# Splitting the even rows of a sequence DFT by s mod 4, and running the DFT sums on zeroed or seeded PSUM banks

## The chip, the cores and the metric

One core of a Trainium2 chip (trn2). The metric is the device time of the core in microseconds, median of several executions. "Step n" below is the n-th of the kernel's 376 equal work steps, counted from 0; it begins with the first TensorE record `H<-Rr,Wc` of that step in the trace. In the profile PE is TensorE and PEld its weight loads, DVE is VectorE, ACT ScalarE, POOL GpSimd, and SPq the queue in which SyncE issues DMAs; `H<-Rr,Wc` means that tile `H` is written from `Rr` and `Wc`. PSUM is the memory that matmuls add into; a bank is one tile of 512 columns of it.

## The reference, cut to what matters

```python
def _attn_ref(x):                      # x: (8, 3008, 256)
    X = np.fft.fft(x, axis=1)          # the s-DFT: over 3008 rows
    X = np.fft.fft(X, axis=2)          # over 256 channels
    return X.real.astype(np.float32)

def _moe_ref(x, w_in, w_out):          # (24064,256), (256,2048), (2048,256)
    h = x @ w_in
    g = h * np.cos(h)
    return (g @ w_out).astype(np.float32)
```

The output is `_moe_ref` of the reshaped `_attn_ref`. The channel DFT is folded into `w_in` at the start of the kernel. What is left per batch is a real and an imaginary DFT over the rows, for even and odd output indices: four "DFTs" (R even, I even, R odd, I odd), each from operands folded by the symmetries of the cosine and the sine.

## The kernel before: the parts that the change touches

Each of 376 steps has 11 fp32 matmuls of 256 columns on TensorE, at least five VectorE operations, seven ScalarE operations and four GpSimd sums (`sum_1` to `sum_4`, of which the third product on bank `pB` needs `sum_2`). In between lie, batch by batch, the loads of `x`, the folds on GpSimd, and the four DFTs, each in two halves (even and odd rows of the folded sequence).

```python
    def load_x(b):                       # [four tiles of 128 partitions x 6 rows]
        for j in (2, 1):                 # reversed row order: a gather by an index table
            c = 1 if j == 2 else 2 if b == NB - 1 else 0
            nc.gpsimd.indirect_dma_start(out=L[j], in_=xflat,
                in_offset=bass.IndirectOffsetOnAxis(ap=ix[:, c : c + 1], axis=0), ...)
        nc.sync.dma_start(out=L[0], in_=xrows(b, 0, 6, 128))
        nc.sync.dma_start(out=L[3], in_=xrows(b, HALF, 6, 128))
    # [...]
    def dft_mms(ps, ri, kodd, par, stat, width):
        n = NO if kodd else NE           # 376 or 377 outputs
        for t in range(3):
            m = 2 * t + par
            c = par * BW + t * NE
            mm(ps[:, 0:n], stat[:, m * width : m * width + 128],
               MC[ri, kodd][:, c : c + n], t == 0, t == 2)   # start flag, stop flag

    def set_rest(ps, n):                 # the zero matmul behind each half
        mm(ps[:, n:512], zero[:, 0:128], zero[:, 0 : 512 - n], False)
    # [...]
    class Dft:
        def copy(self):                  # ScalarE: odd half out of PSUM
            act(self.bs[0:M, 0:n], self.pb[0:M, 0:n])
        def plus(self):                  # VectorE: ring <- odd + even half
            vtt(self.ring[0:M, sl], self.bs[0:M, a:z], self.pa[0:M, a:z], ALU.add)
        def minus(self):                 # VectorE: reversed ring <- even - odd half
            ...
    # [...]
    def load_ext(j):                     # channel 128 of all rows, element by element
        copy(...)                        # 8 x 768 elements of 4 bytes, SyncE queue
        nc.sync.dma_start(out=xe_dr[j], in_=t[:, 0:768])
    def get_ext():                       # and back in runs of six
        for j in range(4):
            nc.sync.dma_start(out=xs[:, j], in_=xe_dr[j].rearrange("b (p m) -> p b m", m=6))
    # [...]
    def at_half(step, d, par, col):      # where a half stands in the schedule
        def run():
            d().ps = bank("H")
            d().mms(par, d().ps)
            set_rest(d().ps, d().n)
        at(t + 4.75, run)
        # odd: copy at t+T+1.46; even: plus, minus at t+T+1.01
```

The banks `H` are shared with the main steps, where ScalarE writes the channel-128 term into the bank and the matmuls add to it without a start flag. A DFT half starts with the start flag, and a zero matmul on the columns behind it follows. Without these zero matmuls the numbers come out wrong (before_no_zero below: relative error 0.24); the reading is that the start flag makes TensorE forget that those columns had been written.

## Time and profile before

| | before |
|---|---|
| time, median of the 3 runs | 2002.85 us (2000.21 to 2002.99) |
| profiled span | 1999.9 us, granted TensorE clock 0.997 |
| PE / DVE / ACT / POOL busy | 99 / 70 / 72 / 67% |
| step 0 begins / steps 28 to the end | 38.9 us / 1815.5 us |

From the page of before, part 1 (busy us, share of the span, instructions) and part 4 (the chain of waits that ended last, by engine):

```profile
PE 1975.4 (99%) x8842; PEld 1648.6 (82%) x8842; DVE 1406.9 (70%) x2278; ACT 1431.2 (72%) x2729; POOL 1336.8 (67%) x1842
...
PE 92%; DVE 2%; issue 2%; ACT 1%; POOL 1%; DMA 1%; DVEq 0%; POOLq 0%; SPq 0%; ACTq 0%
```

TensorE is the bound. Its busy time can't be added up, because the records of pipelined matmuls overlap; the starts can. The timeline of before around one DFT half, TensorE alone (start, length, engine, line, operation, tiles, shapes, count):

```profile
1008.08 0.59 PE L229 MATMUL pD<-G,w 128*128 128x256 f32 x2
1008.51 2.06 PE L229 MATMUL H<-MC,o 128*128 128x376 f32 x6
1010.51 0.23 PE L229 MATMUL H<-zero 1*128 1x136 bf16 x1
1010.66 1.13 PE L229 MATMUL H<-Rr,Wc 128*128 128x256 f32 x4
```

An fp32 matmul is two records. Two of 256 columns go from 1008.08 to 1008.51, 216 ns each; six of 376 columns and the wait for the zero matmul take 2.00 us. Read record by record, a DFT record takes 316 ns, but 409 where the zero matmul follows; the zero matmul 157; the first record behind it 320 instead of 216. That is 93 + 157 + 104 = 354 ns for one zero matmul of 136 columns: its own weight load and that of the fp32 matmul behind it are not hidden (in the trace they start within 4 ns of their matmuls, the other loads about one record earlier).

GpSimd behind a gather of before, timeline:

```profile
181.93 1.00 POOL L288 TENSOR_TENSOR o<-xl 128x381 f32<-128x381 f32 x1
183.20 0.96 POOL L142 DMA_INDIRECT xl<-in_x_dram,ix  x1 [0.27 <-DVE G L598]
184.18 3.03 POOL L238 TENSOR_TENSOR G<-G 128x256 f32<-128x256 f32 x4
```

A gather stands right behind the fold that frees its buffer and holds the four sums of the step back. TensorE's waits for GpSimd in before, from the list of waits (total us, times, longest):

```profile
PEld pB L229 <- POOL G L238: 13.3, 38, 1.0
...
PE pB L229 <- POOL G L238: 1.8, 6, 0.6
```

So there were small waits already.

### The profile page before, as it was taken

What the parts mean: (1) busy time and instruction counts of PE and PEld (TensorE: products, weight loads), DVE (VectorE), ACT (ScalarE), POOL (GpSimd) and SP (SyncE); (2) the same over time, 40 slices, a digit from 0 to 9 for tenths busy, and PEclk for the clock granted to TensorE, in tenths of its full rate; (3) what the DMA queues carried; (4) which work ended last, traced back from release to release, by engine and by line L of the source; (5) the groups of instructions that cost most, each with busy time, mean ns of one, the idle gap of its engine ahead of it and who ended that gap; (6) DMA issues with size and microseconds to landing.
All of it is one profiled execution on the core that took longest, in us unless ns stands there. A gap on an engine that the chain in (4) does not pass through costs nothing.

```text
span 1999.9 us, 27874 instructions
## 1 busy us (share of the span) xinstructions
PE 1975.4 (99%) x8842; PEld 1648.6 (82%) x8842; DVE 1406.9 (70%) x2278; ACT 1431.2 (72%) x2729; POOL 1336.8 (67%) x1842
## 2 busy tenths in 40 slices
PE   8999999999999999999999999999999999999997
PEld 4878888888888888888788888888888888888886
DVE  5776667766677666777677766777667766677776
ACT  2777667776677767777677766777667876677775
POOL 3777657776677756777567865778647776555654
PEclk9999999999999999999999999999999999999999
DMA  9712100211002110130101301013000100001101
GB/s 309 6 34 76 22 12 19 56 41 19 11 19 69 24 23 11 20 83 9 22 18 18 80 9 22 11 28 81 9 16 11 30 19 10 13 11 16 18 11 22
DMA packets 252139, 66.90 MB, mean 33 GB/s; under 512 B 242194, under 2 KB 245034, under 8 KB 251482
## 3 DMA queue, kind: packets, MB, share of 16 engines
q1 hardware_dynamic: 249578, 52.53, 14.4%
q0 software_dynamic: 2416, 12.61, 1.9%
q8 instruction: 70, 1.15, 0.2%
q14 instruction: 75, 0.61, 0.1%
HBM read 40.26 MB, written 24.80 MB: 33 GB/s over the span
## 4 chain that ended last, share of the span: by engine, by line
PE 92%; DVE 2%; issue 2%; ACT 1%; POOL 1%; DMA 1%; DVEq 0%; POOLq 0%; SPq 0%; ACTq 0%
PE H L229 38%; PE pB L229 16%; PE pC L229 16%; PE pD L229 15%; PE pA L229 8%; DVE G L598 1%; POOL G L238 1%; ACT G L241 1%; DVE G L235 0%; DMA wex<-wx 0%; DMA wx<-Ws 0%; ACT E L241 0%; DVE v L235 0%; DVE M L235 0%; POOL xl L142 0%
## 5 line engine op out<-in xcount | busy, mean ns | idle before, releaser
L238 POOL TENSOR_TENSOR G<-G 128x256 f32<-128x256 f32 x1504 | 1079.6, 728 | 619.1 <-DVE G L598 532.5
L598 DVE SCALAR_TENSOR_TENSOR G<-H,G 128x512 f32<-128x512 f32 x376 | 257.4, 685 | 309.1 <-ACT G L241 309.1
L235 DVE TENSOR_TENSOR G<-H,G 128x512 f32<-128x512 f32 x376 | 260.1, 692 | 222.8 <-ACT G L241 219.7
L241 ACT ACTIVATE E<-H 128x512 f32<-128x512 f32 x376 | 224.2, 596 | 261.1 <-PE H L229 257.9
L229 PE MATMUL H<-Rr,Wc 128*128 128x256 f32 x1504 | 393.1, 384 | 4.7 <-ACT H L241 4.6
L241 ACT ACTIVATE G<-H 128x512 int32<-128x512 f32 x376 | 224.5, 597 | 239.3 <-DVE G L235 236.1
L229 PE MATMUL H<-Ir,Ws 127*128 127x256 f32 x1504 | 388.6, 380 | 1.4 <-ACT E L241 1.4
L229 PE MATMUL pC<-G,WT 128*128 128x256 f32 x1504 | 387.0, 379 | 0.6 <-DVE u L235 0.4
L241 ACT ACTIVATE H<-Rb,wex 128x256 f32<-128x256 f32 x752 | 360.2, 479 | 25.8 <-DMA wex<-wx 6.5
L229 PEld LDWEIGHTS H<-Rr,Wc 128*128 128x128 f32 x1504 | 280.0, 190 | 49.7 <-ACT H L241 7.4
L229 PEld LDWEIGHTS H<-Ir,Ws 127*128 127x128 f32 x1504 | 283.0, 190 | 45.6 <-ACT E L241 7.1
L229 PEld LDWEIGHTS pC<-G,WT 128*128 128x128 f32 x1504 | 284.3, 189 | 42.8 <-PE H L229 2.5
L241 ACT ACTIVATE G<-G,halfpi 128x512 f32<-128x512 f32 x376 | 269.1, 716 | 0.3 <-DVE G L235 0.3
L235 DVE TENSOR_TENSOR G<-E,H 128x512 f32<-128x512 f32 x376 | 255.9, 681 | 3.4 <-issue 2.0
L235 DVE TENSOR_TENSOR M<-G,M 128x512 f32<-128x512 f32 x376 | 257.7, 685 | 0.0
L598 DVE SCALAR_TENSOR_TENSOR G<-G,M 128x512 f32<-128x512 f32 x376 | 254.5, 677 | 0.4 <-ACT M L241 0.3
L241 ACT ACTIVATE M<-M,halfpi 128x512 f32<-128x512 f32 x376 | 245.9, 654 | 0.3 <-DVE M L235 0.2
L229 PE MATMUL pB<-G,WT 128*128 128x256 f32 x752 | 227.5, 384 | 1.9 <-POOL G L238 1.8
L229 PE MATMUL pA<-G,w 128*128 128x256 f32 x752 | 223.7, 379 | 0.9 <-PE H L229 0.9
L241 ACT ACTIVATE M<-G 128x512 int32<-128x512 f32 x376 | 224.4, 597 | 0.0
L229 PE MATMUL pD<-G,WT 128*128 128x256 f32 x752 | 223.8, 379 | 0.0
L229 PE MATMUL pD<-G,w 128*128 128x256 f32 x752 | 223.7, 379 | 0.0
(111 smaller groups left out, 1762.2 us busy)
## 6 DMA issues: line engine op xcount, KB each, us to landing
out_dram<-ot SPq DMA_DIRECT2D x504, 32.0 KB
xl<-in_x_dram SPq DMA_DIRECT2D x16, 768.0 KB
MC<-dft_mats SPq DMA_DIRECT2D x4, 1131.0 KB
out_dram<-ot SPq DMA_DIRECT2D x256, 2.0 KB
Rb<-r SPq DMA_DIRECT2D x10, 376.0 KB
w<-in_moe_w_in_dram SPq DMA_DIRECT2D x4, 512.0 KB
w<-in_moe_w_out_dram SPq DMA_DIRECT2D x1, 2048.0 KB
out_dram<-ot SPq DMA_DIRECT2D x64, 28.0 KB
```

What stands on the lines that cost most here:

```text
L229: nc.tensor.matmul(out_, lhsT=lhsT, rhs=rhs, start=start, stop=stop, skip_group_check=True)
L235: pin(nc.vector.tensor_tensor(out=o, in0=a, in1=b, op=op))
L238: pin(nc.gpsimd.tensor_tensor(out=o, in0=a, in1=b, op=op))
L241: pin(nc.scalar.activation(out=o, in_=i, func=func, **kw))
L598: nc.vector.scalar_tensor_tensor(out=o, in0=h, scalar=TWO_PI, in1=c, op0=ALU.mult, op1=ALU.mult)
```

## The change

Intent: (1) the even half of each DFT is split once more, by s mod 4, so that 189 outputs are computed for each of two blocks and the rest come by adding and subtracting: 4 matmuls of 189 columns in place of 3 of 377. (2) No start flag on `H` banks: the even half runs on a bank that VectorE zeroed, the odd half on a bank that ScalarE seeded with the unfolded even half, so the sum comes out of PSUM directly, and the zero matmuls go. (3) For that the rows lie differently on the partitions: runs of four rows, and runs of two, so each load becomes two or three.

```diff
+def _row_of(m):
+    p = np.arange(128)
+    return 4 * p + m if m < 4 else 512 + 4 * (p % 64) + 2 * (p // 64) + m - 4
 [...]
         for j in (2, 1):
-            c = 1 if j == 2 else 2 if b == NB - 1 else 0
-            nc.gpsimd.indirect_dma_start(out=L[j], ...)
-        nc.sync.dma_start(out=L[0], in_=xrows(b, 0, 6, 128))
-        nc.sync.dma_start(out=L[3], in_=xrows(b, HALF, 6, 128))
+            runs = ((4 if j == 1 and b == NB - 1 else 2 * j - 2, slice(2 * ND, 6 * ND)),
+                    (2 * j - 1, slice(0, 2 * ND)))
+            for c, part in runs:
+                nc.gpsimd.indirect_dma_start(out=L[j][:, part], ...)
+        for j, row in ((0, 0), (3, HALF)):
+            nc.sync.dma_start(out=L[j][:, 0 : 4 * ND], in_=xrows(b, row, 4, 128, 4))
+            for h in range(2):
+                nc.sync.dma_start(out=L[j][64 * h : 64 * h + 64, 4 * ND :],
+                                  in_=xrows(b, row + 512 + 2 * h, 4, 64, 2))
 [...]
+    def dft_parts(ri, kodd, par):
+        if par:                          # odd rows: three matmuls of n columns, as before
+            [...]
+        else:                            # tile 4 twice: low and high partitions masked
+            for t, m in enumerate((0, 4, 2, 4)):
+                yield m, t // 2 * NH, mats[:, t * NH : (t + 1) * NH]
 [...]
-    def set_rest(ps, n):
-        mm(ps[:, n:512], zero[:, 0:128], zero[:, 0 : 512 - n], False)
 [...]
+        def clear(self):
+            self.uv = bank("H")
+            pin(nc.vector.memset(self.uv[:, 0 : 2 * NH], 0.0))
+        def side(self):                  # ScalarE: the second block out of PSUM
+            act(self.vs, self.uv[:, NH : 2 * NH])
+        def unfold(self):                # VectorE: even half = u + v, reversed u - v
+            vtt(self.ab[:, 0:n1], u[:, 0:n1], v[:, 0:n1], ALU.add)
+            vtt(self.ab[:, n - 1 : n - 189 : -1], u[:, 0:188], v[:, 0:188], ALU.subtract)
+        def seed(self):                  # ScalarE: even half into the odd half's bank
+            self.pb = bank("H")
+            act(self.pb[:, 0:n], self.ab[:, 0:n])
+        def plus_sum(self):              # ScalarE: ring <- bank
+        def minus_sum(self):             # VectorE: reversed ring <- 2 * even - bank
 [...]
+        at(t + 2.905, lambda: d().clear())
+        at(t + 4.75, lambda: d().first_part())
+        at(t + T + 1.46, lambda: d().side())
+        at(u + 1.01, lambda: d().unfold())
+        at(u + 2.95, lambda: d().seed())
+        at(u + 4.75, lambda: d().second_part())
+        at(u + T + 1.01, lambda: d().minus_sum())
+        at(u + T + 1.46, lambda: d().plus_sum())
 [...]
-                nc.sync.dma_start(out=xs[:, j], in_=xe_dr[j].rearrange("b (p m) -> p b m", m=6))
+                nc.sync.dma_start(out=xs[:, j, :, 0:4], ...)     # channel 128: three small
+                for h in range(2):                               # loads in place of one
+                    nc.sync.dma_start(out=xs[64 * h : 64 * h + 64, j, :, 4:6], in_=pairs[h])
```

That seeding works follows from the Trainium skill ("PSUM — Partial Sum Buffer", The four PSUM rules): writes of VectorE and ScalarE don't touch the written-bits, and a matmul without the start flag adds where the bit is set.

## The prediction

> **What bounds the kernel.** TensorE's own stream. The page gives PE 99% busy and the chain of waits 92% PE. Busy sums overlap, so I read the starts in the timeline of single instructions: an fp32 matmul shows as two records, 216 ns apart for 256 columns and 316 ns for 377 (columns x 2 / 2.4 GHz + about 2 ns). A normal step is 22 records, 4.75 us, x376 = 1787 us. After the first 55 us all starts that lag this spacing add up to about 14 us apart from those around zero matmuls; VectorE (70%), ScalarE (72%) and GpSimd (67%) have slack.
>
> **Removed from PE.**
> 1. Zero matmuls after each DFT half. In the timeline at 1010 us the last DFT record to the zero matmul takes 409 instead of 316 ns, the zero matmul 157, the first record after it 320 instead of 216: 0.354 us each, because the weight loads around it are exposed (104 ns, 93 ns). 56 + 1 go: 20 us.
> 2. The even half: 6 records of 377 columns (6 x 316 = 1.90 us) become 8 of 189. Estimate 189 x 2 / 2.4 + 2.5 = 160 ns each, 1.28 us, if the weight load stays hidden. Two exposed loads in the trace start 108 ns apart; the Trainium skill ("TensorE: Matmul & The Clock Gate", LDWEIGHTS) gives columns / 1.2 GHz = 107 ns, which agrees. 108 < 160, so it should. 0.62 us x 28 = 17 us; the channel-128 DFT 1.2 us more.
> 3. Startup: 5 DFTs also shrink, but before 39 us PE waits for the small `wex` DMA, so only R_odd and I_odd count: about 1 us, partly eaten by longer loads and VectorE work.
>
> Sum: about 39 us, on the critical path.
>
> **Added, off PE.** Per DFT, costed from the 377-column operations (480 ns): VectorE a memset of 378 columns (about 0.4 us), two unfolds of 189 (0.3 us each), one subtraction left of two: about +0.5 us. ScalarE: side 0.3, seed 0.48, plus 0.48 in place of one 0.48 copy: about +0.8 us. These fall into gaps: before a DFT's first matmul ScalarE's last `ext` ended mostly 1.03 us earlier, VectorE's g_minus 1.16 us. In 4 of 28 first halves g_minus ends only 0.06 us before it; there the memset should stall PE about 0.5 us. Together 2 us lost.
>
> GpSimd: the gathers double, 4 per batch, each 0.96-1.0 us whatever the bytes (my assumption). They sit before the sums that mm_X1 waits for; those sums now end 1.1 us early in the median, but around gathers 0.05 to 0.6 us early, with stalls of 0.3-0.4 us already. 12 places in the loop x 0.4-0.95 us: 6 us lost. The GpSimd part of the extra channel: 1 us.
>
> **Net** 39 - 9 = 30 us less: **1971 us, range 1959 to 1987.** Chances: faster by over 2% 0.27, within 2% 0.72, slower 0.01.
>
> **What would show it.** (1) Last DFT record to next H<-Rr at normal spacing, no zero group except three for the middle rows. (2) Even DFT records 160 ns apart; 190 would mean that the weight load binds, costing 7 us. (3) pB<-G,WT waiting for GpSimd near 1 us after gathers. (4) First DFT matmuls delayed after memset or seed only in a few places; a third-bank wait (ScalarE's `ext` for VectorE) no longer than before.
>
> **What would make it wrong.** Weight loads not hidden at 189 columns; waits on VectorE or ScalarE exposing a 104 ns load at each DFT; half-row gathers much cheaper or spread apart (then 1964 or less, near the 2% edge); VectorE/ScalarE falling behind because DFT steps, shorter by 1 us, no longer let them catch up (then 1985).

## More of the kernel before

The SyncE queue of before while the channel-128 loads are issued (timeline; SPq is the queue of DMA issues):

```profile
25.39 0.36 SPq L149 DMA_DIRECT2D xl<-in_x_dram  x1
25.85 0.38 SPq L150 DMA_DIRECT2D xl<-in_x_dram  x1
26.28 35.68 SPq L434 DMA_DIRECT2D x<-in_x_dram  x4
```

The element-wise loads of channel 128 (`x<-in_x_dram`) keep that queue busy for 36 us, most of it two of the four. The last of the reads that end this chain (`xs<-xe_dr`) was issued at 95.3 us, and TensorE wanted the result at 102.3 us.

## The result, and the profile after

| | before | after |
|---|---|---|
| time, median | 2002.36 us (4 runs, 2000.21 to 2002.99) | 1989.72 us (4 runs, 1986.49 to 1994.85) |
| ratio | | 0.994 (0.9923 to 0.9958) |
| profiled span | 1999.9 us | 1993.1 us |

The kernel became 12.6 us faster by the medians, not 30. The four runs, 1986.5, 1987.2, 1992.3 and 1994.9 us, spread over 8.4 us; those of before over 2.8 us. The profiled run was the slowest of the four, so its stretches show the losses at their largest. Where the time went, from the first TensorE record of the steps named (us):

| stretch | before | predicted change | after | after, profiled again |
|---|---|---|---|---|
| start to step 0 | 38.9 | 0 | 39.9 | 42.8 |
| steps 0 to 11 | 58.4 | -1 | 58.8 | 59.9 |
| steps 11 to 17 (channel 128) | 34.4 | 0 (-1.2 + 1) | 47.1 | 36.8 |
| steps 17 to 28 | 52.6 | 0 | 53.3 | 53.3 |
| step 28 to the end | 1815.5 | -29 | 1794.0 (-21.5) | 1794.1 (-21.4) |

The page of after, the lines that answer to those of before:

```profile
PE 1940.6 (97%) x8855; PEld 1654.5 (83%) x8855; DVE 1417.0 (71%) x2343; ACT 1452.1 (73%) x2790; POOL 1352.9 (68%) x1860
...
PE 82%; DMA 4%; DVE 4%; POOL 4%; ACT 2%; issue 2%; SPq 2%; DVEq 0%; POOLq 0%
```

The chain of waits is no longer TensorE almost alone: 4% DMA, 4% VectorE, 4% GpSimd, 2% the SyncE queue. The matmuls of the even halves in the loop went as planned. Timeline of after, an even half:

```profile
1001.00 1.45 PE L256 MATMUL H<-MC,o 128*128 128x189 f32 x8
1002.28 1.02 PE L256 MATMUL H<-Rr,Wc 128*128 128x256 f32 x4
```

Eight records take 1.28 us, 160 ns each, and the next step follows at once, with its first weight load hidden. GpSimd, timeline of after, at the second gathering place of batch 2 (the place shown for before):

```profile
195.99 1.00 POOL L315 TENSOR_TENSOR o<-xl 128x381 f32<-128x381 f32 x1
197.26 0.96 POOL L162 DMA_INDIRECT xl<-in_x_dram,ix  x1 [0.27 <-POOL o L315]
198.53 0.96 POOL L162 DMA_INDIRECT xl<-in_x_dram,ix  x1 [0.30 <-DVE G L262]
199.50 3.03 POOL L265 TENSOR_TENSOR G<-G 128x256 f32<-128x256 f32 x4
```

and TensorE's waits for GpSimd in after, from the list of waits:

```profile
PEld pB L256 <- POOL G L265: 26.4, 41, 2.9
...
PE pB L256 <- POOL G L265: 13.2, 14, 2.5
```

Each gather takes 0.94 to 1.0 us in the loop, with 6 KB for each partition in before and 4 or 2 KB here, and comes with another 0.3 us in front, so the second one starts 1.27 us behind the first. Summed over the starts of the records from step 28 on, TensorE's starts in front of the third product (`pB<-G,WT`) lag 14.1 us in after and 3.6 us in before: 10.5 us lost to the additional gathers, for which I had put 6. In after the lag at the 12 places behind gathers is 0.69 to 2.63 us each; the longest, in the last batch, contains 1.1 us in which GpSimd waits for a gather to land before it issues a small correcting load.

The other loss is in the SyncE queue. Timeline of after:

```profile
26.08 0.35 SPq L170 DMA_DIRECT2D xl<-in_x_dram  x1
26.48 1.11 SPq L174 DMA_DIRECT2D xl<-in_x_dram  x2
27.69 0.53 SPq L170 DMA_DIRECT2D xl<-in_x_dram  x1
31.10 2.98 SPq L174 DMA_DIRECT2D xl<-in_x_dram  x2
37.22 32.23 SPq L527 DMA_DIRECT2D x<-in_x_dram  x4
```

Six loads of batch 1 stand in front of channel 128 instead of two, and the queue waits for earlier transfers in between; the list of waits of after for the queue alone has

```profile
SPq L527 <- DMA MC<-dft_mats: 3.1, 1, 3.1
SPq L174 <- DMA w<-in_moe_w_out_dram: 2.9, 1, 2.9
SPq L174 <- DMA MC<-dft_mats: 2.0, 1, 2.0
```

These waits are not in the list of before. Channel 128 starts at 37.2 us instead of 26.3, and has twelve small reads at its end instead of four. The timeline of after where it ends:

```profile
107.15 1.28 SPq L554 DMA_DIRECT2D xs<-xe_dr  x2
...
110.50 0.38 POOL L265 TENSOR_TENSOR xs<-xs 128x96 f32<-128x96 f32 x1 [8.29 <-DMA out_dram<-ot]
110.96 0.53 POOL L265 TENSOR_TENSOR xe<-xs 128x48 f32<-128x48 f32 x2
...
111.30 4.18 PE L256 MATMUL H<-MC,xe 128*8 128x189 f32 x28 [7.48 <-POOL xe L265]
```

The last two reads are issued at 107.15 and 107.79 us; GpSimd's fold of them starts at 110.50 (the releaser named, an output DMA, is issued after the fold's own reads; the reads are what it needs), and TensorE stands 7.5 us. Then it is slow for a while: over 100 to 124 us the granted clock is 0.79, and the channel's DFT behind the stall takes 4.11 us instead of 2.02, so the 7.5 us cost 9.6 by step 12. "Profiled again" (run after_again below) had no such stall, so these 9.6 us are not in every run. The 3.1 us that steps 12 to 16 take beyond before are another matter: after_again has 2.5 of them without the stall, and channel_rows below shows where they come from.

### The profile page after: what moved, and what is told of

It reads as the page before. It is cut to its first block, busy times and chain, and to the rows that moved or that the text cites. A ratio compares the mean times of both kernels' runs of the same rounds, so it can differ in the third digit from the quotient of the medians.

```text
span 1993.1 us, 28143 instructions
## 1 busy us (share of the span) xinstructions
PE 1940.6 (97%) x8855; PEld 1654.5 (83%) x8855; DVE 1417.0 (71%) x2343; ACT 1452.1 (73%) x2790; POOL 1352.9 (68%) x1860
## 4 chain that ended last, share of the span: by engine, by line
PE 82%; DMA 4%; DVE 4%; POOL 4%; ACT 2%; issue 2%; SPq 2%; DVEq 0%; POOLq 0%
PE H L256 33%; PE pC L256 14%; PE pB L256 14%; PE pD L256 14%; PE pA L256 7%; DMA x<-in_x_dram 2%; POOL G L265 2%; DVE G L705 1%; ACT G L268 1%; SPq L527 1%; DVE G L262 1%; DMA pick<-pick_mats 1%; POOL xl L162 1%; DVE v L262 1%; DMA xl<-in_x_dram 1%
## 5 line engine op out<-in xcount | busy, mean ns | idle before, releaser
L256 PE MATMUL H<-Rr,Wc 128*128 128x256 f32 x1504 | 387.9, 380 | 7.6 <-ACT H L268 7.6
L256 PEld LDWEIGHTS H<-Rr,Wc 128*128 128x128 f32 x1504 | 284.3, 190 | 56.5 <-ACT H L268 10.4
L262 DVE TENSOR_TENSOR G<-E,H 128x512 f32<-128x512 f32 x376 | 255.0, 678 | 12.6 <-PE H L256 10.4
L256 PE MATMUL pB<-G,w 128*128 128x256 f32 x752 | 223.7, 379 | 0.0
```

The costliest lines, as they stand in the source:

```text
L256: nc.tensor.matmul(out_, lhsT=lhsT, rhs=rhs, start=start, stop=stop, skip_group_check=True)
L262: pin(nc.vector.tensor_tensor(out=o, in0=a, in1=b, op=op))
```

## The experiments

Theories. **G**: the doubled gathers on GpSimd cost 11 us in the loop. **C**: the channel's loads come late because of the longer SyncE queue, and cost 0 to 10 us from run to run. Rivals stand with each run. Times of before in the same rounds: 2003.89 us for gathers_apart, no_gathers, before_no_zero and ext_early; 2002.41 for before_cleared, after_again, halves_merged and merged_apart; 2002.17 for before_split_gathers, banks_swapped, channel_rows and all_tuned. Twelve kernels ran.

### gathers_apart: the gathers moved into steps without folds

```diff
-                nc.gpsimd.indirect_dma_start(...)          # hoisted right behind the fold
+                if b < 2: gather()
+                else: gathers.append(lambda g=gather: pin(g()))
 [...]
+            for n in range(5 if b == NB - 1 else 4):       # one per step, no folds there
+                at((l0 + min(n, 3)) * T + 1.3, lambda n=n: state["gathers"][n]())
```

> The kernel after, with the four gathers of each batch from the third on kept one per step in four steps without folds, instead of two and two right behind a fold; same count, same bytes. Gather theory: GpSimd has 1.7 us free in such a step and a gather takes 1.0 us, so the waits of the third product for GpSimd after gathers (12 places, 12.9 us in the profile of after, about 1.7 us in that of before) nearly vanish: 10 to 12 us faster than after, 1977 to 1980 us. Rival (doubling the gathers costs little, the GpSimd waits come from VectorE being late): no more than 3 us gained.

Measured: 1977.19 us (1975.59 to 1978.62), ratio 0.9869; 12.5 us below the first result of after. In its profile step 28 to the end takes 1782.8 us, 11.2 less than after, and the starts of the third product lag 3.7 us instead of 14.1. The timeline of gathers_apart on GpSimd:

```profile
252.10 1.00 POOL L164 DMA_INDIRECT xl<-in_x_dram,ix  x1
255.18 3.02 POOL L277 TENSOR_TENSOR G<-G 128x256 f32<-128x256 f32 x4 [2.09 <-DVE G L717]
```

The same gathers now lie in idle time; behind one GpSimd waits 2.09 us for VectorE. G holds; the rival is out.

### no_gathers: plain loads of as many bytes in their place (wrong numbers on purpose)

```diff
+            if b > 1:                                      # forward rows: wrong order
+                nc.sync.dma_start(out=L[j][:, 2 * ND :], in_=xrows(b, row, 4, 128, 4))
+                [... two more for the runs of two]
+                continue
```

> Wrong numbers on purpose: the kernel after, with the gathers of batches 2 to 7 replaced by plain loads of as many bytes in forward row order, issued by SyncE. Gather theory: GpSimd loses 24 gathers of about 1 us, the stalls behind them vanish as in the run with gathers kept apart: 1977 to 1980 us. If gathers kept apart gains and this one doesn't, the transfers matter and not GpSimd's issue time. Rival as there: no more than 3 us gained.

Measured: 1979.11 us (1975.65 to 1981.78), ratio 0.9871. As fast as gathers_apart within the noise, with the bytes still moved: what cost time was GpSimd's issue, not the transfer. In the profile its loop takes 3.0 us more than that of gathers_apart; one wait of GpSimd for a plain load in the last batch, 3.2 us, accounts for it.

### before_split_gathers: the cost added to the kernel before

```diff
-            nc.gpsimd.indirect_dma_start(out=L[j], ... ix[:, c : c + 1] ...)
+            for h in range(2):
+                k = c + 3 * h
+                nc.gpsimd.indirect_dma_start(out=L[j][:, 3 * h * ND : (3 * h + 3) * ND],
+                                             ... ix[:, k : k + 1] ...)
```

> The kernel before with each gather of six rows split into two gathers of three rows; same bytes and rows, twice the gathers (right numbers). Gather theory: 12 more gathers of 0.96 us in the loop stand behind a fold, where the sums were already late or had at most 0.6 us to spare: 6 to 10 us slower than before, 2008 to 2013 us. If a gather's time went with its bytes, or GpSimd were not what TensorE waits for there: within 2 us of before.

Measured: 2013.48 us (2010.71 to 2014.04), ratio 1.0058; 11.3 us slower than before, a little over the range. Its waits for GpSimd, from the list of waits:

```profile
PEld pB L232 <- POOL G L241: 24.0, 42, 1.9
...
PE pB L232 <- POOL G L241: 10.5, 14, 1.5
```

These are nearly the figures of after, with nothing else of the change in the kernel.

### before_no_zero: the zero matmuls alone, taken out (wrong numbers on purpose)

```diff
             d().mms(par, d().ps)
-            set_rest(d().ps, d().n)
```

> Wrong numbers on purpose: the kernel before without the zero matmul after each of its 56 DFT halves; nothing else differs. My count (0.354 us each, of which 0.2 us are weight loads left uncovered): 56 x 0.354 = 20 us less, 1982 to 1984 us. Rival (other engines set the pace of the DFT steps once TensorE is shorter there, so that the gain is lost): 10 us or less, 1992 us or more.

Measured: 1982.64 us (1979.63 to 1986.37), ratio 0.9896: 21 us, as counted (56 x 0.354 = 20). The rival, other engines setting the pace once TensorE is shorter there, is out.

### before_cleared: zero matmuls replaced by memsets, with right numbers

```diff
-            d().mms(par, d().ps)
-            set_rest(d().ps, d().n)
 [... dft_mms can leave out the start flag]
+        def clear():
+            d().ps = bank("H")
+            pin(nc.vector.memset(d().ps[:, 0 : d().n], 0.0))
+        at(t + 2.905, clear)
+        at(t + 4.75, lambda: d().mms(par, d().ps, False))
```

> One part of the change alone, with right numbers: the kernel before with VectorE zeroing each DFT half's bank and no zero matmul; same matmuls, loads and gathers otherwise. Zero matmuls cost 20 to 21 us (the run without them); in 8 of the 56 halves g_minus ends within 0.06 us of the first matmul, so the memset stalls TensorE there, 8 x 0.45 = 4 us: 1985 to 1989 us. Rival (VectorE can't take 56 memsets of 0.37 us without setting the pace): 1992 us or more.

Measured: 1987.15 us (1986.54 to 1994.92), ratio 0.9934. Step 28 to the end takes 4.5 us more than without any memset (before_no_zero). This one part of the change, with no new row layout, does at least as well as the whole change (1989.72 and 1992.8 us in its two measurements).

### ext_early: channel 128 first in the queue

```diff
     for j in range(4):
-        at(-T, lambda j=j: load_ext(j))
+        at(-2 * T, lambda j=j: load_ext(j))
```

> The kernel after, with the four loads of channel 128 put into SyncE's queue before the loads of batch 1 instead of behind them; nothing else differs. Late-channel theory: in the profile of after, step 12 of TensorE begins 9.6 us later against before than step 11 does, and steps 13 to 16 lose 3.1 us more, because these loads were issued 11 us later than before; with them first, that loss (12.7 us of the profiled run, about 8 us of the median) goes: 1979 to 1983 us, a spread of the runs under 3 us, and no wait of the channel's DFT for its operands. Rival (the loss is the work of the channel's twelve small loads and of GpSimd, not the place in the queue): under 3 us gained, 1987 us or more.

Measured: 2004.27 us (2000.95 to 2005.44), ratio 1.000. A miss: slower than after by 14.6 us by the medians. The stall before the channel's DFT was gone (0.09 us), but the loads of batch 1 now stood behind 55 us of the channel's loads and writes (the first was issued at 80.6 us), and GpSimd waited for them (timeline of ext_early):

```profile
96.46 0.19 POOL L336 COPY e<-xl 128x6 f32<-128x6 f32 x1 [10.13 <-DMA xl<-in_x_dram]
...
100.76 1.22 PE L256 MATMUL pB<-G,WT 128*128 128x256 f32 x2 [9.21 <-POOL G L265]
```

The stall moved to whatever came second in the queue. The place in the queue decides who waits, so C's mechanism is supported; its remedy was wrong. The 3.1 us of steps 13 to 16, which the expectation also put down to the late channel, did not go: steps 12 to 16 take 25.1 us here, 25.6 in after and 22.5 in before.

### after_again: the kernel after once more

No edit.

> The kernel after, unchanged, to see how it spreads. Late-channel theory: the channel's loads end at about the moment when TensorE wants them, so runs fall anywhere from no loss to about 8 us: 1986 to 1995 us, spread 5 us or more, and the profile shows a stall before the channel's DFT between 0 and 8 us with the last of its loads landing just before it. Rival (the stall of 7.6 us is in every run): median 1990 us, spread under 3 us, the same stall in this profile.

Measured: 1992.8 us (1988.66 to 1997.76, 6 runs), ratio 0.9955. The spread is 9 us. In this profile the channel's last read was issued at 100.6 us, TensorE wanted the DFT at 107.7, and there was no stall; but step 0 began at 42.8 us. The rival (the same stall in every run) is out. All 14 profiles fit one line within 0.5 us: the stall is the issue of the last read + 3.5 us - the time at which TensorE gets there, where that is positive. The five with the start of before or after unchanged:

| run | last read issued | TensorE there | stall |
|---|---|---|---|
| before | 95.3 | 102.3 | 0.1 |
| after | 107.8 | 103.6 | 7.6 |
| after_again | 100.6 | 107.7 | 0.1 |
| gathers_apart (same start) | 103.1 | 106.5 | 0.1 |
| no_gathers (same start) | 104.3 | 104.8 | 3.2 |

With the same code at the start, the last read falls between 100.6 and 107.8 us and step 0 between 39.9 and 42.8. In every profile step 0 begins 1.1 us after the small `wex` DMA has landed (37.8 us in before, 38.8 in after, 41.7 in after_again), as the prediction said; what it did not see is that `wex` itself would come later.

### halves_merged: fewer loads in the queue

Rows 512 to 767 dealt in order, so a tile takes two loads instead of three.

```diff
-    return 4 * p + m if m < 4 else 512 + 4 * (p % 64) + 2 * (p // 64) + m - 4
+    return 4 * p + m if m < 4 else 512 + 2 * p + m - 4
 [...]
-    low = np.arange(128) < 64
+    low = np.arange(128) % 2 == 0
 [... and the two half loads made one, for x and for the channel]
```

> The kernel after, with rows 512 to 767 dealt to partitions in pairs in order (row 512 + 2p instead of two halves of 64 partitions); the masks become even and odd partitions. That leaves 4 loads of x instead of 6 per batch in SyncE's queue, and 8 small loads of the channel instead of 12. Late-channel theory: the channel's first load is issued some us earlier than 37 us, its last one 3 us or more earlier than 107.8 us, and the stall before its DFT is under 1 us: 1984 to 1987 us, spread under 4 us. Rival (the single-element loads alone set the time): the stall stays as in after_again, 1988 us or more.

Measured: 1989.15 us (1986.27 to 1992.96), ratio 0.9933, against 0.9955 for after in the same rounds. The mechanism came out as expected: the channel's first load at 29.0 us instead of 36 to 37, no stall before its DFT, and step 0 at 37.9 us (37.9 to 38.4 in the four later kernels with this layout). The time didn't, a miss: steps 0 to 11 took 62.7 us instead of 58.8 to 59.9, and the spread was 6.7 us. Where, the next runs show.

### merged_apart: both

> Both: rows dealt in order as in halves_merged, and gathers one per step as in gathers_apart (the last batch's patch in a step of its own). If both causes are independent: gathers 11 to 12 us, the channel 3 to 5 us below after: 1973 to 1976 us, clear of 2% only in part. It should be the fastest kernel so far.

The edits are those of halves_merged and gathers_apart. Measured: 1975.31 us (1972.50 to 1981.04), ratio 0.9866. A hit. What is left in steps 0 to 11 is this, in the timeline of merged_apart, TensorE alone:

```profile
57.09 1.19 PE L266 MATMUL pA<-G,w 128*128 128x256 f32 x2 [2.35 <-issue]
58.07 1.06 PE L266 MATMUL pB<-G,w 128*128 128x256 f32 x2
```

TensorE stands 2.35 us in front of its first product on bank `pA`, although "issue" is all that the view can name; then each pair takes 0.86 us instead of 0.43. The wait itself is not new: after, after_again and gathers_apart have the same 2.35 us at this place, before 0.95. New is the half speed behind it, which those three do not have; why it falls into some kernels and not into others is not shown.

### banks_swapped: another bank for the last DFT of batch 0

```diff
-        (T + 3.1, lambda: I_odd.first("pD")),
-        (T + 3.2, lambda: I_odd.second("pA")),
+        (T + 3.1, lambda: I_odd.first("pA")),
+        (T + 3.2, lambda: I_odd.second("pD")),
```

> The kernel merged_apart with the two accumulator banks of the first batch's last DFT (I, odd) swapped, so that the bank that TensorE wants first (pA) is read early and the one read last is pD. In merged_apart TensorE stands 2.35 us at 57 us for pA, until VectorE's second ring write from it ends at 57.0 us, and the nine records behind it are 0.21 us apart over the normal spacing (half clock). If the unfold's place in VectorE's queue is the cause of the loss in step 2 to 3 (3.0 us against before), the wait and the slow records go: step 3 begins 2.5 to 3.5 us earlier against step 2, total 1971.5 to 1973. Rival (VectorE itself is late there, whatever the bank): the wait moves to pD or the sums, under 1 us gained.

Timeline of banks_swapped at the same place:

```profile
54.81 0.67 PE L266 MATMUL pA<-G,w 128*128 128x256 f32 x2 [0.65 <-ACT E L278]
55.32 0.59 PE L266 MATMUL pB<-G,w 128*128 128x256 f32 x2
```

The wait is down to 0.65 us and the slow pairs are gone; steps 0 to 11 take 58.4 us instead of 62.7. So VectorE's reads of `pA`, later by the unfold, were the cause of the wait. Yet the time is 1975.45 us (1972.72 to 1978.02), ratio 0.9863: not faster, a miss. In the profile the gain is handed back at once: TensorE reaches the channel at 101.7 us, the last read is issued at 101.9, and steps 11 to 17 take 43.9 us instead of 37.5 (stall 3.6 us, then a slow stretch). The profiled run was the slowest of the four (1978.02 us); two of the others, 1972.72 and 1973.17, are near the range expected, but they have no profile.

### channel_rows: the channel's extra row operations

```diff
-            [128, 2 * NH], FP, tag=f"xt{par}", bufs=1, name=f"xt{par}"
+            [128, 2 * NH], FP, tag=f"xt{par}", bufs=2, name=f"xt{par}"
 [...]
-    at(14 * T + 1.35, lambda: ext_rows(1, gtt))
+    at(14 * T + 1.0, lambda: ext_rows(1, vtt))
```

> The kernel merged_apart with two buffers for the channel's side copies and the channel's second rows on VectorE instead of GpSimd. In merged_apart ScalarE waits 1.7 and 0.6 us for those buffers in step 13, and TensorE 2.4 us for ScalarE at the start of step 14; then GpSimd's four row operations (2.9 us) hold the sums back 1.7 us, and the late rows TensorE 1.6 us at step 16. If these extra row operations are the cause: 3.5 to 5.5 us less, 1970 to 1972. Rival (the loss at steps 14 and 16 is that of before, there from the start): under 1.5 us.

Measured: 1972.66 us (1969.17 to 1975.27), ratio 0.9852. Steps 11 to 17 take 35.0 us instead of 37.5. So the extra row operations are most of the 2.4 to 3.1 us that every kernel with the change loses there without any late load. By the medians the gain, 2.7 us, is not clear of the noise, and it is a miss: smaller than expected, because the rows still make the sums late twice (0.6 us each) and the ring's copy of them 1 us.

### all_tuned: both mends

> Both mends on top of merged_apart. If independent: 6 to 9 us less than merged_apart, 1966 to 1969; faster than before by 1.6 to 1.8%, not quite 2%.

Measured: 1971.76 us (1970.00 to 1977.33, 4 runs), ratio 0.9858: a miss, 1966 to 1969 was expected. It has the lowest median of all, but its interval (0.9843 to 0.9874) overlaps that of channel_rows. Its profile (1967.1 us) has every stretch of the start at or under that of before: 37.9, 58.4, 34.3 us. One of the four runs (1977.33) lies 7 us above the lowest; that may be the late channel again, but that run wasn't profiled.

## Why the prediction was wrong

The prediction said 1971 us, 1959 to 1987; the kernel took 1989.72. Point by point:

- **Zero matmuls, 20 us: right.** before_no_zero gained 21 us, and the exposed weight loads behind the halves are gone in the profile after.
- **Even half, 17 us: right on TensorE.** The records are 160 ns apart; the weight load stays hidden, as the Trainium skill's 107 ns ("TensorE: Matmul & The Clock Gate", LDWEIGHTS) let expect.
- **Memset in four places, 0.5 us each, 2 us together: right.** Timeline of after at one of them:

```profile
236.63 0.37 DVE L445 MEMSET H<- 128x378 f32 x1
...
237.06 1.55 PE L256 MATMUL H<-MC,o 128*128 128x189 f32 x8 [0.28 <-DVE H L445]
```

  TensorE starts 0.44 to 0.54 us late there, 2.0 us in all.
- **"two unfolds of 189 (0.3 us each)" on VectorE, "These fall into gaps": not quite, about 2.5 us lost.** The starts of a later product (`pC`) lag 3.0 us in all where they lagged 1.2 in before. It is not the memsets: before_cleared has eight of their stalls and still 1.2. At the four places where the lag doubles the unfold stands in VectorE's queue in front of the read that frees `pC`, and at four others it is new, 0.2 us each. Timeline of after at one of the first, VectorE and TensorE:

```profile
724.53 0.35 DVE L262 TENSOR_TENSOR ab<-H,vs 128x189 f32<-128x189 f32 x1
724.79 0.34 DVE L262 TENSOR_TENSOR ab<-vs,H 128x188 f32<-128x188 f32 x1
725.05 0.41 DVE L262 TENSOR_TENSOR u<-v,pC 128x256 f32<-128x256 f32 x1
725.61 1.10 PE L256 MATMUL pC<-G,WT 128*128 128x256 f32 x4 [0.28 <-DVE u L262]
```

  After a wait of either kind the next DFT has one record 0.1 us late, 0.8 us in all. In the loop without gather stalls the gain is 32.7 us (gathers_apart) of the 37 counted.
- **Gathers, "12 places x 0.4-0.95 us: 6 us lost": this step failed, in its size.** It measured 10.5 us in the loop by TensorE's starts, 10.6 and 12.5 us by the medians of the two ways of taking it away (11.2 in the loop of gathers_apart, which the luck of the channel does not touch) and 11.3 us by adding it to before. I had taken the issue alone, 0.96 us, and not the 0.3 us in front of each, and of my own range, 4.8 to 11.4 us, a value near the low end. The wait of the third product for GpSimd "near 1 us after gathers" did appear.
- **"Startup ... about 1 us" gained and the channel "1.2 us more" against "1 us" lost: this step failed, and here a mechanism was missing.** I costed the added operations of TensorE, VectorE, ScalarE and GpSimd and left out the added DMAs of the SyncE queue: three loads for one. They pushed the channel's 36 us of element-wise loads back by 11 us, into the time when TensorE wants them: 9.6 us by step 12 in the profile of after, nothing in that of after_again. The start up to step 0 took another 1 to 4 us. Halving the added loads brought step 0 to 37.9 us and ended the stall in that profile; putting the channel first moved the stall to the loads behind it.
- **The sizes in the same step were off too.** The channel's DFT gained nothing where 1.2 us were counted. TensorE in before and in after_again:

```profile
102.38 2.09 PE L229 MATMUL H<-MC,xe 128*8 128x377 f32 x24
107.75 2.09 PE L256 MATMUL H<-MC,xe 128*8 128x189 f32 x28
```

  From its first start to that of the next step it takes 2.02 us in both: the four small DFTs of the channel write different partitions, and their records start mostly in bunches, some ns apart, so their lengths do not add up as I had added them. The added side copies and rows cost 2.5 to 3 us in steps 12 to 16, where 1 us was counted; channel_rows took 2.5 us of steps 11 to 17 away by rearranging them. And in steps 0 to 11, "about 1 us" gained became 0.4 to 1.5 us lost: the wait for `pA` grew from 0.95 to 2.35 us with the unfold (banks_swapped).
- "What would make it wrong" named VectorE or ScalarE falling behind and unhidden weight loads. The loads stayed hidden at 189 columns, and VectorE was late only by the small amounts above. The DMA queue wasn't on the list.

The two failed steps, with VectorE's small part, account for the miss: about 5 us of gathers beyond the estimate, 2 to 3 us of VectorE in the loop, and 9 to 15 us before step 17 (from the stretches above: after_again +7.8 us, after +14.1, where -1 was predicted). Where the median falls is in part luck: ten runs of after range from 1986.5 to 1997.8 us, and the two that were profiled differ by 9.6 us at the channel alone. Left open: which of the single, unprofiled runs had the channel's stall, and why step 0 begins anywhere from 39.9 to 42.8 us with the same code.

## What to carry to other kernels

When a change alters a data layout, count the DMA instructions it adds per queue and look up who stands behind them in that queue: a load that is one of three now can cost a wait of a quite different consumer, 70 us later. A gather cost its engine about 1.3 us per instruction here, with 2, 4 or 6 KB for each partition, so place it in steps where that engine has idle time instead of where its buffer happens to come free. And on a bound engine, a tiny instruction of another type and shape can cost more than twice its own spacing: here 0.35 us for a matmul of 136 columns with 0.157 us of its own. Taking these out alone, with memsets in their place, gained 15 us with right numbers, at least as much as the whole change.

## What the Trainium skill lacked or had wrong

- "TensorE: Matmul & The Clock Gate", Back-to-back issue gap: this section has no gap for fp32 matmuls. Here an fp32 matmul is two records, each columns x 2 / 2.4 GHz + 2 to 3 ns apart: 160 ns for 189 columns, 216 for 256, 316 for 377.
- The same page, Part 2, says that weight loads are pulled ahead of running matmuls, with conditions on row groups and the background buffer but none on the type or length of the matmuls: between fp32 matmuls the load was hidden down to 189 columns, but before a bf16 matmul of one row it was not (93 ns), nor before the fp32 one behind it (104 ns).
- The same page, Part 1, gives an idle window of about 3.4 us for the half clock. Here a gap of 2.35 us was followed by pairs at half speed in merged_apart, while the same gap of 2.35 us at the same place in gathers_apart was not.
- "DMA: Bandwidth & Descriptors", Latency and other measured facts, gives about 1 us of first-byte latency for DMAs that GpSimd issues, but not how long an indirect one keeps GpSimd from its other work: 0.94 to 1.0 us in the loop, the same for 2, 4 and 6 KB for each partition, and 0.3 us in front of it.
- The same page, Rules for kernel authors, says that a non-contiguous last dimension becomes one descriptor per element; the runs add what that does to the queue: four such loads in a row, of at most 6144 elements each, kept SyncE's queue busy for 28 to 41 us over the 14 profiles, most of it two of them, and the DMAs behind them waited.
- "PSUM — Partial Sum Buffer", Summary: its table says that a seed by VectorE or ScalarE must be 0. The kernel after seeds a bank 28 times with nonzero values and is correct; the page's own rule 2 allows this where no start flag has cleared the bits.
